# Output weights in 28 contiguous rows per partition, the attention output re-laid through HBM, and five last transfers: a decode step of attention and a gated feed-forward on one core

## The chip, the cores and the metric

The kernel runs on one core of a Trainium2 chip. The metric is the device time of one execution in microseconds (us), the median of several runs; lower is better.

## The reference

One token `x` (1 x 448) is normalised (mean and variance, no weights) to `xn`, and three terms are added: `x`, an attention over a cache, and a block `B` of the mixture kind that, with one token to choose from, always chooses it.

```
q = (xn @ wq) in 16 heads of 256;  k, v = caches of 8 heads, 65536 positions, 256 wide (two q heads share one)
p = softmax(q . k / 16) over the 65536 positions;   o = p @ v          (16 x 256)
A = o.reshape(4096) @ wo                                                (wo: 4096 x 448)
B = xn + sigmoid(xn @ w_r) * ((silu(xn @ w_gate) * (xn @ w_up)) @ w_down)
out = x + A + B
```

Everything in HBM is bf16. Keys and values are 268 MB each, of 549 MB that are read in all; each byte is used once.

## The kernel before, in words

**Units.** The 65536 positions of a head lie 512 to a partition. A unit is 128 of them per partition (8.4 MB of keys or values), so a head has `U` = 4 units, and there are `NU` = 32 key units and 32 value units. Three slots of one large tile `ring` hold units: keys alternate between slots 0 and 1, values come through slot 2. Within a unit, TensorE transposes keys (`k_T`), multiplies them with q (`k_QK`), and the scores are turned back to positions on partitions (`k_JT`); after a head's last key unit the softmax follows, and then four units of values (`pe_V`), which lag the keys by one head. `NT` = 28 value units belong to heads 0 to 6, the last four (`NT` to `NT + 3`) to head 7, in `ending()`.

**Queues.** Each engine has a list of its operations in program order, written out by hand: `O` records an operation, `W` a wait for another one, `item` a transfer that SP issues, with what SP waits for ahead of it. SP issues all large transfers in one order. Its last ones are: value unit `NT` to slot 0; gate and up weights (`wg`), down weights (`wd`) and output weights of heads 0 to 6 (`wo`) to slot 2, which holds no values at that time; value unit `NT + 1` to slot 1, `NT + 2` to slot 0; unit `NT + 3` to slot 2, in the parts of `LAST`, after `SUM`, the last use of the weights there; the rest of `wo` (`wx`, after `HT`); and head 7's output weights in three parts (`wo_end`, waits `we0` to `we2`).

**The attention output.** For heads 0 to 6, `oT_all` (and its sum over units, `oT_f`) has feature 2p + f of a head on partition p. The weights `wo` come with four consecutive rows of a head's 512 on each partition (`wo_rows`: "(h p f) n -> p h f n"), so each of the two q heads of a pair takes half of the partitions. `REGROUP` brings `oT_f` into that layout: 16 small products with strided columns of the identity, each to a half of the partitions. `OTH` copies the result to `oT_h` in bf16. `ATTN` then adds 26 products of a column of `oT_h` with 448 columns of `wo` in `ps_a`; the last two rows per partition of head 6 come later as `wx` and are added in `FIN_X`.

**Behind it on TensorE**: `FFN1G`, `FFN1` (gate and up), `HTP`, `FFN2` (down); on VectorE `YS`, `YX`, and `SUM`, which adds `ps_a`. Then the values of unit `NT + 1`, `FIN_BASE`, units `NT + 2` and `NT + 3`. Between the parts of `NT + 3`, `WARM` puts products whose results are not used. The last `DIRECT` parts are multiplied with the values as the stationary side ("direct"), so that `OB` (the copy of `ps_o`) can be made from the parts before. Then `OT`, `OTSB`, `FIN_X` and the three `FIN` with head 7's weights, `RESULT`, and the transfer of the output.

All TensorE products are recorded at line 413, in a helper, and all transfers at line 903; so readings go by tile: `ps_q` with `oT_h` is ATTN, `ps_t` with `xnT_sb` FFN1, `ps_t` with `hT_sb` FFN2, `ps_o` the values. `kt_all L826` on DVE is SUM.

Of the kernel before, what the change touches and what calls it, by code (L numbers as in the profile page):

```python
# [4 lines left out]
BF16 = mybir.dt.bfloat16  # L5
# [5 lines left out]
NKT = 4  # L11
NSLOT = 3
CH = 64
HC = 2
LAST = [64, 32, 16, 8, 4, 4]
DIRECT = 2
NF = 4
WARM = {0: (5, 512), 1: (2, 512), 2: (1, 512), 3: (1, 256)}
ACT_M = (3,)
TORD = (3, 0, 1, 2)  # L20

# [1 line left out]
def bass_parallel_sum__gqa_block_cached__moe_arch_mod__decode_kernel(  # L23
# [20 lines left out]
    P = 128  # L44
    _, Hkv, Sk, Dh = A_k_cache.shape
    D = A_x.shape[-1]
    HqDh = A_wq.shape[1]
    Hq = HqDh // Dh
    rep = Hq // Hkv
    F = B_w_gate.shape[1]  # L50
    NH = Dh // P
# [3 lines left out]
    FK = F // P  # L55
# [20 lines left out]
    SLOT = HC * CH * Dh  # L76
    HALF = CH * Dh
    WQN, WGN, WDN, WON = RP * HqDh // 2, RP * F, FH * D, rep * NH * D
    FO = rep * NH
    WOA = (Hkv - 1) * WON  # L80
    WEN = WOA + WGN + 2 * WDN
    assert WEN + 2 * D <= SLOT
# [3 lines left out]
    def S_(name, shape, dtype):  # L86
        t = nc.sbuf_tensor(name, shape, dtype)
        sb.append(t)
        return t.__enter__()

    ring = S_("ring", [P, NSLOT * SLOT], BF16)
    kt_all = S_("kt_all", [P, NKT * 8 * P], BF16)
# [3 lines left out]
    wo_all = slots[2][:, 0:WOA]  # L96
# [35 lines left out]
    rs = S_("rs", [P, NH, rep], FP32)  # L132
    oT_all = S_("oT_all", [P, NH, NT, rep], FP32)
    oT_f = S_("oT_f", [P, NH, Hkv - 1, rep], FP32)
    oT_h = S_("oT_h", [P, FO, Hkv - 1], BF16)
    KB = 2 * FB
    sg_sb = [kt_all[0:2, c * KB:(c + 1) * KB].bitcast(FP32) for c in range(2)]
    h_sb = kt_all[0:2, 2 * KB:3 * KB]
# [1 line left out]
    DQ = D // NF  # L140
    FROWS = 32 * (NF - 1) + 1
    res_bf = kt_all[0:FROWS, 3 * KB + 2 * D:3 * KB + 2 * D + DQ]
    wo_x = kt_all[:, 2 * KB:2 * KB + WON // 2]
    assert WON // 2 <= KB and WON <= 2 * KB and 3 * KB + 2 * D + DQ <= NKT * 8 * P
    hT_sb = S_("hT_sb", [P, FH, 2], BF16)
    ob_sb = S_("ob_sb", [P, 2 * Dh], BF16)
    oT_sb = S_("oT_sb", [P, NH, rep], BF16)
# [19 lines left out]
    ps_m = PS_("ps_m", [P, 512], FP32)  # L167
    C_XNT, C_BC, C_TOT, C_OT, C_Q, C_BIG = 0, 16, 18, 22, 28, 64
    C_HT = C_Q
    assert C_Q + NH * Hq + 4 <= C_BIG and C_HT + FK <= C_BIG and C_BIG + P <= 512  # L170

    sems = {}
    handles = []
# [4 lines left out]
        sems[name] = s.__enter__()  # L178
        return name

    for n_ in ["pe", "act", "dve", "pool", "qk", "jt", "evq", "exp", "pc", "qc", "sc", "w0", "out", "wq", "wg", "wo", "wd", "we0", "we1", "we2", "wx", "half0", "half1"]:
        SEM(n_)
    for i in range(NTB):
        SEM(f"ev{i}")
# [23 lines left out]
    def W(e, *key):  # L208
        put(e, "w", key, None, None)
# [3 lines left out]
    def O(e, key, fn, sem=None, n=1):  # L213
        key = key if isinstance(key, tuple) else (key,)
        if not ghost[0]:
            weight[key] = n
        put(e, "o", key, fn, sem or e)
# [21 lines left out]
    def item(key, parts, need=()):  # L239
        for n in need:  # L240
            W("sp", *n)
        for ap, src, sem in parts:
            semtot[sem] = semtot.get(sem, 0) + 16
            items[key] = (sem, semtot[sem])
            prog["sp"].append(("d", here[0], ("DMA", key, len(prog["sp"])), (ap, src), sem))
# [22 lines left out]
    def wo_view(t):  # L268
        return t.rearrange("p (i f n) -> p i f n", i=rep, f=NH)

    def wo_rows(h0, h1):

        return A_wo[h0 * rep * Dh:h1 * rep * Dh, :].rearrange("(h p f) n -> p h f n", p=P, f=FO)

    def wo_at(h, f):
        return wo_all[:, (h * FO + f) * D:(h * FO + f + 1) * D]

    def k_item(u):
        need = [("FREE", u - 2)] if u >= 2 else ()
# [13 lines left out]
    for t in range(1, NT):  # L293
        v_item(t)
        if t + U + 1 < NU:
# [1 line left out]
    slot_item("v", NT, 0, None, [("FREE", NU - 2)])  # L297
    item("wg", [(wg_area[:, 0:WGN // 2], flat_src(B_w_gate, F), "wg"), (wg_area[:, WGN // 2:WGN], flat_src(B_w_up, F), "wg")], [("VFREE", NT - 1)])
    item("wd", [(wd_area.rearrange("p (s x) -> p s x", s=2), B_w_down.rearrange("(s p t) n -> p s (t n)", s=2, p=P), "wd"), (x_again, A_x[0], "wd")])
    HL = Hkv - 2  # L300
    item("wo", [(wo_all[:, 0:HL * WON].rearrange("p (h x) -> p h x", h=HL), wo_rows(0, HL).rearrange("p h f n -> p h (f n)"), "wo"),
                (wo_all[:, HL * WON:HL * WON + WON // 2], wo_rows(HL, HL + 1)[:, 0, 0:FO // 2, :].rearrange("p f n -> p (f n)"), "wo")])
    slot_item("v", NT + 1, 1, None, [("FREE", NU - 1)])
    slot_item("v", NT + 2, 0, None, [("VFREE", NT)])
    slot_item("v", NT + 3, 2, [("last%d" % k if k < len(LAST) - 1 else "slot2", J) for k, J in enumerate(LAST)], [("SUM",)])
    item("wx", [(wo_x, wo_rows(HL, HL + 1)[:, 0, FO // 2:FO, :].rearrange("p f n -> p (f n)"), "wx")], [("HT",)])
    ENDS = [(0, 0, NH), (1, 0, 1), (1, 1, NH)]
    for k, (i, f0, f1) in enumerate(ENDS):
        item(("wo_end", k), [(wo_view(wo_end)[:, i, f0:f1, :], wo_src()[:, i, f0:f1, :], "we%d" % k)])
# [102 lines left out]
    def mm(*a, **k):  # L412
        return pe.matmul(*a, **k)  # L413
# [242 lines left out]
    def pe_attn():  # L656
        W("dve", "OTSB", NT - 1)
        for hf in range(NH):
            O("dve", ("OTF", hf), lambda it, hf=hf: nc.vector.tensor_reduce(
                out=oT_f[:, hf, :, :], in_=oT_all[:, hf, :, :].rearrange("p (h t) i -> p h i t", t=U), axis=AX.X, op=ALU.add))  # L660
        W("dve", "OTF", NH - 1)
        W("pe", "OTF", NH - 1)
        HN = Hkv - 1

        def regroup(it):

            for i in range(rep):
                for r in range(rep):
                    for hf in range(NH):
                        c = C_BIG + (r * NH + hf) * HN  # L670
                        ins = mm(ps_m[i * P // rep:(i + 1) * P // rep, c:c + HN], lhsT=ident_f[:, r:P:rep], rhs=oT_f[:, hf, :, i],
                                 start=True, stop=True, tile_position=(0, i * P // rep))
            return ins

        O("pe", "REGROUP", regroup)
        W("dve", "REGROUP")
        O("dve", "OTH", lambda it: nc.vector.tensor_copy(
            out=oT_h[:, :, :], in_=ps_m[:, C_BIG:C_BIG + FO * HN].rearrange("p (f h) -> p f h", f=FO)))
        W("pe", "OTH")
        W_item("pe", "wo")  # L680
        todo = [(h, f) for h in range(HN) for f in range(FO) if h < HN - 1 or f < FO // 2]
        O("pe", "ATTN", lambda it: [mm(ps_a, lhsT=oT_h[:, f, h:h + 1], rhs=wo_at(h, f),
                                       start=(h, f) == todo[0], stop=(h, f) == todo[-1]) for h, f in todo][-1])

    def pe_ffn1():
        W_item("pe", "wg")
# [101 lines left out]
    def fin(rows, o, col, first=False, last=False):  # L788
        for g in range(NF):
            ins = mm(ps_s[32 * g:32 * g + 1, 0:DQ], lhsT=col, rhs=rows[:, o + g * DQ:o + (g + 1) * DQ], start=first,  # L790
                     stop=last, tile_position=(0, 32 * g), skip_group_check=True)
        return ins
# [5 lines left out]
    def ending():  # L798
        here[0] = ("S", 1)
        T = NU - 1  # L800
        n = NU * SETS
        k_JT(n - 2)
        k_QK(n - 1)
        k_JT(n - 1)
        pe_m1t(T)
        pe_bc(T)
        W("pe", "OTSB", NT - 1)
        values(NT)
        pe_tot(NT)
        pe_attn()  # L810
        pe_ffn1()
        pe_ffn_hT()
        pe_ffn2()
        W_item("dve", "wd")
        O("dve", "XN_AGAIN", lambda it: nc.vector.tensor_scalar(out=xn_again, in0=x_again, scalar1=stat[0:1, 7:8], scalar2=stat[0:1, 4:5],
                                                                op0=ALU.add, op1=ALU.mult))
        W("dve", "XN_AGAIN")
        W("dve", "FFN2")
        W("dve", "ATTN")
        W("dve", "SIG")  # L820
        O("dve", "YS", lambda it: nc.vector.scalar_tensor_tensor(  # L821
            out=sum_f, in0=ps_y, scalar=stat[0:1, 6:7], in1=xn_again, op0=ALU.mult, op1=ALU.add))
        W("dve", "YS")
        O("dve", "YX", lambda it: nc.vector.tensor_tensor(out=sum_f, in0=sum_f, in1=x_again, op=ALU.add))
        W("dve", "YX")
        O("dve", "SUM", lambda it: nc.vector.tensor_tensor(out=sum_f, in0=ps_a, in1=sum_f, op=ALU.add))  # L826
        values(NT + 1)
        W("pe", "SUM")
        W("pe", "SCOPY", T)

        O("pe", "FIN_BASE", lambda it: fin(sum_f, 0, ones_f[0:1, 0:1], first=True))
        O("pe", "OT_ZERO", lambda it: mm(ps_m[0:P, C_OT:C_OT + NH * rep], lhsT=s2[0][:, 0:P], rhs=zero_bf[:, 0:NH * rep], start=True, stop=True,
                                         skip_group_check=True))
        values(NT + 2)
        values(NT + 3)
        dve_ob(T)
        pe_oT(T)
        W_item("pe", "wx")

        def fin_x(it):  # L840
            for f in range(FO // 2):
                ins = fin(wo_x, f * D, oT_h[:, FO // 2 + f, HL:HL + 1])
            return ins

        O("pe", "FIN_X", fin_x)
        W("pe", "OTSB", T)
        for k, (i, f0, f1) in enumerate(ENDS):
            W_item("pe", ("wo_end", k))

            def f(it, k=k, i=i, f0=f0, f1=f1):  # L850
                for hf in range(f0, f1):
                    ins = fin(wo_end, (i * NH + hf) * D, oT_sb[:, hf, i:i + 1], last=k == len(ENDS) - 1 and hf == f1 - 1)
                return ins

            O("pe", ("FIN", k), f)
        W("dve", "FIN", len(ENDS) - 1)
        O("dve", "RESULT", lambda it: nc.vector.tensor_copy(out=res_bf, in_=ps_s[0:FROWS, 0:DQ]))
        W("sp", "RESULT")
        prog["sp"].append(("d", here[0], ("OUT", 0), (out[0, 0].rearrange("(g n) -> g n", g=NF), res_bf[0:FROWS:32, :]), "out"))
# [272 lines left out]
```

## Time and profile before

| | |
|---|---|
| median of 3 runs | 1277.01 us (1277.01 to 1277.2) |
| profiled execution | 1278.14 us |
| its span, first to last instruction | 1275.5 us |
| read from HBM | 549.03 MB, 430 GB/s over the span |
| granted TensorE clock, mean | 0.881 |
| busy: PE, DVE, ACT | 965.2, 570.5, 436.1 us |
| DMA packets | 12890 |

Times are on the profiled execution's own axis, from the start of its span. PE is TensorE, DVE VectorE, ACT ScalarE; a queue is a list of transfers (q1 is fed by SP, q10 by ACT), which 16 DMA engines work off in packets. "idle before" and square brackets name what an engine waited for last. Rows of the DMA view give packets, megabytes and the time that the packets took as a share of 16 engines over the window.

### The profile page before, as it was taken

How to read it: one execution, taken by the hardware profiler on the slowest of the kernel's cores; microseconds unless marked ns; L12 is line 12 of the kernel's file. 1: busy time of each engine (PE TensorE's matmuls, PEld its weight loads, DVE VectorE, ACT ScalarE, POOL GpSimd, SP SyncE). 2: the span in 40 equal slices, each digit the busy share in tenths (PEclk: the TensorE clock that was granted, in tenths of full speed). 3: DMA queues.
4: the chain of work that ended last, by engine and by line, in shares of the span. 5: the costliest groups of instructions: out<-in, count | busy, mean ns of one | idle time of the engine just before them, and what ended most of it. 6: DMA issues, size and time to landing. Idle time of an engine off the chain costs nothing.

```text
span 1275.5 us, 23552 instructions
## 1 busy us (share of the span) xinstructions
PE 965.2 (76%) x9760; PEld 632.0 (50%) x9760; DVE 570.5 (45%) x1078; ACT 436.1 (34%) x655; POOL 8.0 (1%) x38
## 2 busy tenths in 40 slices
PE   3998988678777779777778776787777698777664
PEld 3676655445444455444455444554454555444331
DVE  4665544445434455343454444453444544444310
ACT  1554433244322434233333243343333334322300
POOL 2000000000000000000000000000000000000000
PEclk9998998889888889887898888898888988888877
DMA  9999999999999999999999999999999999999998
GB/s 404 430 435 433 441 430 434 432 430 444 430 432 436 428 440 434 432 434 432 430 442 432 432 436 430 438 436 430 434 432 430 442 432 432 436 430 436 418 438 357
DMA packets 12890, 549.20 MB, mean 431 GB/s; under 512 B 1355, under 2 KB 1998, under 8 KB 3406
## 3 DMA queue, kind: packets, MB, share of 16 engines
q1 hardware_dynamic: 12874, 549.04, 99.7%
q8 instruction: 8, 0.13, 0.0%
q14 instruction: 4, 0.03, 0.0%
q10 hardware_dynamic: 4, 0.00, 0.0%
HBM read 549.03 MB, written 0.00 MB: 430 GB/s over the span
## 4 chain that ended last, share of the span: by engine, by line
DMA 78%; PE 18%; ACT 2%; issue 1%; DVE 1%; SPq 0%; ACTq 0%; DVEq 0%
DMA ring<-in_A_v_cache_dram 68%; PE ps_o L413 12%; DMA ring<-in_A_k_cache_dram 5%; PE ps_t L413 3%; DMA kt_all<-in_A_wo_dram 3%; DMA ring<-in_A_wo_dram 2%; PE ps_q L413 2%; ACT kt_all L474 2%; PE ps_m L413 1%; SPq L903 0%; DVE kt_all L472 0%; ACT S_sb L555 0%; DVE kt_all L715 0%; PE ps_s L413 0%; DVE kt_all L821 0%
## 5 line engine op out<-in xcount | busy, mean ns | idle before, releaser
L413 PE MATMUL ps_t<-ident_f,ring 128*128 128x128 f32 x4096 | 591.2, 287 | 78.0 <-DMA ring<-in_A_k_cache_dram 56.4
L472 DVE COPY kt_all<-ps_t 128x1024 bf16<-128x1024 bf16 x768 | 487.3, 685 | 291.4 <-PE ps_q L413 286.3
L413 PEld LDWEIGHTS ps_t<-ident_f,ring 128*128 128x128 f32 x4096 | 454.9, 144 | 230.2 <-issue 135.1
L474 ACT ACTIVATE kt_all<-ps_t 128x1024 bf16<-128x1024 bf16 x256 | 261.9, 1023 | 502.2 <-PE ps_q L413 502.1
L413 PE MATMUL ps_o<-ring,p_sb 128*4 128x512 bf16 x2044 | 179.6, 513 | 201.7 <-DMA ring<-in_A_v_cache_dram 197.4
L413 PEld LDWEIGHTS ps_o<-ring,p_sb 128*4 128x4 bf16 x2044 | 54.6, 102 | 289.6 <-issue 264.1
L413 PE MATMUL ps_q<-kt_all,q_cur 128*2 128x512 bf16 x2056 | 164.3, 396 | 0.4 <-DVE kt_all L472 0.4
L496 ACT ACTIVATE s<-ps_q 98x512 bf16<-98x512 f32 x257 | 151.6, 590 | 1.3 <-PE ps_q L413 1.3
L578 DVE RECIPROCAL rs<-ps_m 128x4 f32<-128x4 f32 x29 | 5.3, 183 | 271.6 <-PE ps_m L413 271.6
L565 ACT ACTIVATE p_sb<-S_sb 128x128 bf16<-128x128 bf16 x64 | 18.9, 307 | 262.6 <-PE ps_o L413 262.3
L413 PEld LDWEIGHTS ps_s<-sel_bf,s 128*128 128x128 bf16 x1032 | 64.6, 98 | 5.2 <-ACT s L496 1.9
L413 PE MATMUL ps_s<-sel_bf,s 128*128 128x8 bf16 x1032 | 63.6, 167 | 1.3 <-ACT s L496 1.3
L631 DVE CAST ob_sb<-ps_o 100x512 bf16<-100x512 f32 x29 | 20.1, 692 | 92.4 <-PE ps_o L413 92.4
L413 PEld LDWEIGHTS ps_q<-kt_all,q_cur 128*2 128x2 bf16 x2056 | 26.4, 79 | 44.5 <-issue 44.5
L413 PEld LDWEIGHTS ps_m<-rowsum,ones_f 128*128 128x128 f32 x58 | 12.4, 266 | 23.5 <-issue 23.5
L474 ACT ACT_TABLE_LOAD x7 | 9.0, 1283 | 26.0 <-PE ps_q L413 26.0
L525 DVE TENSOR_REDUCE m1p<-S_sb (+1 forms) x33 | 13.9, 422 | 4.4
L413 PE MATMUL ps_m<-rowsum,ones_f 128*128 128x4 f32 x58 | 14.9, 328 | 0.0
L523 DVE CAST S_sb<-ps_s 128x256 f32 (+1 forms) x33 | 13.7, 415 | 1.9 <-PE ps_s L413 1.9
L555 ACT ACTIVATE S_sb<-S_sb,negmax 128x512 bf16<-128x512 bf16 x16 | 13.2, 851 | 3.2 <-DVE negmax L549 3.2
L413 PE MATMUL ps_m<-diag,ones_f 2*128 2x2 f32 x58 | 11.2, 260 | 3.8 <-DVE diag L540 1.1
L413 PEld LDWEIGHTS ps_m<-diag,ones_f 2*128 2x128 f32 x58 | 8.7, 187 | 10.7 <-DVE diag L540 10.7
(95 smaller groups left out, 132.8 us busy)
## 6 DMA issues: line engine op xcount, KB each, us to landing
ring<-in_A_k_cache_dram SPq DMA_DIRECT2D x10, 4096.0 KB, 28.7
ring<-in_A_v_cache_dram SPq DMA_DIRECT2D x1, 4096.0 KB, 26.5
ring<-in_A_wq_dram SPq DMA_DIRECT2D x1, 3584.0 KB, 11.3
ring<-in_A_wo_dram SPq DMA_DIRECT2D x1, 2688.0 KB, 27.6
ring<-in_A_v_cache_dram SPq DMA_DIRECT2D x1, 2048.0 KB, 30.7
ring<-in_B_w_gate_dram SPq DMA_DIRECT2D x1, 1568.0 KB, 16.2
ring<-in_B_w_up_dram SPq DMA_DIRECT2D x1, 1568.0 KB, 19.6
ring<-in_B_w_down_dram SPq DMA_DIRECT2D x1, 1568.0 KB
```

The lines of the kernel that those rows point to most:

```text
L413: return pe.matmul(*a, **k)
L472: O(e, ("EV", s, m), lambda it: nc.vector.tensor_copy(out=kt[:, :], in_=tb[:, :]), f"ev{m}")
L474: O(e, ("EV", s, m), lambda it: nc.scalar.activation(out=kt[:, :], in_=tb[:, :], func=ACTF.Copy), f"ev{m}")
L496: O("act", ("EVQ", s), lambda it: nc.scalar.activation(out=s2[s % 2][0:QROWS, :], in_=ps_q[0:QROWS, :], func=ACTF.Copy), "evq")
L523: O("dve", ("SCOPY", u), lambda it: nc.vector.tensor_copy(out=S_sb[:, at(it, SBN), :], in_=ps_sn), "sc")
L525: O("dve", ("SMAX", u), lambda it: nc.vector.tensor_reduce(out=m1p[:, :, at(it, 1)], in_=S_sb[:, at(it, SBN), :].rearrange("p n i -> p i n ...
L555: O("act", ("EXP", h, i), lambda it, i=i: nc.scalar.activation(out=S_sb[:, :, i], in_=S_sb[:, :, i], func=ACTF.Exp, bias=negmax[:, i:i + 1 ...
L565: O("act", ("PC", t, c), lambda it: nc.scalar.activation(out=p_sb[:, c, :, :], in_=S_sb[:, n:n + CH, :], func=ACTF.Copy), "pc")
L578: O("dve", ("RS", t), lambda it: nc.vector.reciprocal(out=rs[:, :, :], in_=ps_m[0:P, C_TOT:C_TOT + NH * rep]))
L631: O("dve", ("OB", t), lambda it: nc.vector.tensor_copy(out=ob_sb[0:OROWS, :], in_=ps_o[0:OROWS, :]))
```

## The change

The output weights of heads 0 to 6 (3584 rows) are read as 28 contiguous rows per partition: 26 of them in `wo`, one transfer, and the last two in `wx`. Element 28p + f of the attention output then has to be on partition p. `REGROUP` and `OTH` are replaced: two transposes (`OTROW`) put `oT_f` in 14 rows of 256, `OROW` copies them to `o_row` (a part of `kt_all`) in bf16, ACT writes them to `o_flat` in HBM, waits for that (`oh0`), and reads them back as 128 runs of 28 elements into `oT_h` (`oh1`), for which TensorE waits ahead of `ATTN`. The last value unit comes in five parts and not six: 64, 32, 16, 8 and 8 positions per partition, of which the last is "direct" (before: two of 4). One of the `WARM` entries goes.

```diff
-LAST = [64, 32, 16, 8, 4, 4]
-DIRECT = 2
+LAST = [64, 32, 16, 8, 8]
+DIRECT = 1
+WX = 2
-WARM = {0: (5, 512), 1: (2, 512), 2: (1, 512), 3: (1, 256)}
+WARM = {0: (5, 512), 1: (2, 512), 2: (1, 512)}
...
-    FO = rep * NH
+    FR = (Hkv - 1) * rep * Dh // P
...
-    oT_h = S_("oT_h", [P, FO, Hkv - 1], BF16)
+    oT_h = S_("oT_h", [P, FR], BF16)
+    o_flat = nc.dram_tensor("o_flat", [(Hkv - 1) * rep, Dh], BF16).ap()
...
-    wo_x = kt_all[:, 2 * KB:2 * KB + WON // 2]
+    wo_x = kt_all[:, 2 * KB:2 * KB + WX * D]
+    o_row = kt_all[0:(Hkv - 1) * rep, 2 * KB:2 * KB + Dh]
...
-        return A_wo[h0 * rep * Dh:h1 * rep * Dh, :].rearrange("(h p f) n -> p h f n", p=P, f=FO)
+        return A_wo[0:(Hq - rep) * Dh, :].rearrange("(p f) n -> p f n", f=FR)[:, f0:f1, :].rearrange("p f n -> p (f n)")
...
-    item("wo", [(wo_all[:, 0:HL * WON].rearrange("p (h x) -> p h x", h=HL), wo_rows(0, HL).rearrange("p h f n -> p h (f n)"), "wo"),
-                (wo_all[:, HL * WON:HL * WON + WON // 2], wo_rows(HL, HL + 1)[:, 0, 0:FO // 2, :].rearrange("p f n -> p (f n)"), "wo")])
+    item("wo", [(wo_all[:, 0:(FR - WX) * D], wo_rows(0, FR - WX), "wo")])
...
-    item("wx", [(wo_x, wo_rows(HL, HL + 1)[:, 0, FO // 2:FO, :].rearrange("p f n -> p (f n)"), "wx")], [("HT",)])
+    item("wx", [(wo_x, wo_rows(FR - WX, FR), "wx")], [("HT",)])
...
-        W("pe", "OTF", NH - 1)
-        HN = Hkv - 1
-        def regroup(it):
...
-        O("pe", "REGROUP", regroup)
-        W("dve", "REGROUP")
-        O("dve", "OTH", lambda it: nc.vector.tensor_copy(
-            out=oT_h[:, :, :], in_=ps_m[:, C_BIG:C_BIG + FO * HN].rearrange("p (f h) -> p f h", f=FO)))
-        W("pe", "OTH")
+        HR = (Hkv - 1) * rep
+        for hf in range(NH):
+            W("pe", "OTF", hf)
+            O("pe", ("OTROW", hf), lambda it, hf=hf: mm(ps_m[0:HR, C_BIG + hf * P:C_BIG + (hf + 1) * P],
+                                                        lhsT=oT_f[:, hf, :, :].rearrange("p h i -> p (h i)"), rhs=ident_f[:, :],
+                                                        is_transpose=True, start=True, stop=True))
+        W("dve", "OTROW", NH - 1)
+        O("dve", "OROW", lambda it: nc.vector.tensor_copy(
+            out=o_row.rearrange("r (p f) -> r f p", f=NH), in_=ps_m[0:HR, C_BIG:C_BIG + NH * P].rearrange("r (f p) -> r f p", f=NH)))
+        W("act", "OROW")
+        for k, (dst, src) in enumerate(((o_flat, o_row), (oT_h[:, :], o_flat.rearrange("r d -> (r d)").rearrange("(p f) -> p f", f=FR)))):
+            items["oh", k] = ("oh%d" % k, 16)
+            prog["act"].append(("d", here[0], ("DMA", "oh", k), (dst, src), "oh%d" % k))
+            if k == 0:
+                W("act", "DMA", ("oh", 0))
+        W("pe", "DMA", ("oh", 1))
         W_item("pe", "wo")
-        todo = [(h, f) for h in range(HN) for f in range(FO) if h < HN - 1 or f < FO // 2]
-        O("pe", "ATTN", lambda it: [mm(ps_a, lhsT=oT_h[:, f, h:h + 1], rhs=wo_at(h, f),
-                                       start=(h, f) == todo[0], stop=(h, f) == todo[-1]) for h, f in todo][-1])
+        O("pe", "ATTN", lambda it: [mm(ps_a, lhsT=oT_h[:, f:f + 1], rhs=wo_all[:, f * D:(f + 1) * D],
+                                       start=f == 0, stop=f == FR - WX - 1) for f in range(FR - WX)][-1])
...
-            for f in range(FO // 2):
-                ins = fin(wo_x, f * D, oT_h[:, FO // 2 + f, HL:HL + 1])
+            for f in range(WX):
+                ins = fin(wo_x, f * D, oT_h[:, FR - WX + f:FR - WX + f + 1])
```

More of the change, by code (lines that the diff above doesn't have):

```diff
@@ L142, in bass_parallel_sum__gqa_block_cached__moe_arch_mod__decode_kernel @@
     res_bf = kt_all[0:FROWS, 3 * KB + 2 * D:3 * KB + 2 * D + DQ]
-    wo_x = kt_all[:, 2 * KB:2 * KB + WON // 2]
-    assert WON // 2 <= KB and WON <= 2 * KB and 3 * KB + 2 * D + DQ <= NKT * 8 * P
+    wo_x = kt_all[:, 2 * KB:2 * KB + WX * D]
+    o_row = kt_all[0:(Hkv - 1) * rep, 2 * KB:2 * KB + Dh]
+    assert WX * D <= KB and Dh <= KB and WON <= 2 * KB and 3 * KB + 2 * D + DQ <= NKT * 8 * P
     hT_sb = S_("hT_sb", [P, FH, 2], BF16)
@@ L169, in bass_parallel_sum__gqa_block_cached__moe_arch_mod__decode_kernel @@
     C_HT = C_Q
-    assert C_Q + NH * Hq + 4 <= C_BIG and C_HT + FK <= C_BIG and C_BIG + P <= 512
+    assert C_Q + NH * Hq + 4 <= C_BIG and C_HT + FK <= C_BIG and C_BIG + NH * P <= 512
     sems = {}
@@ L179, in SEM @@
         return name
-    for n_ in ["pe", "act", "dve", "pool", "qk", "jt", "evq", "exp", "pc", "qc", "sc", "w0", "out", "wq", "wg", "wo", "wd", "we0", "we1", "we2", "wx", "half0", "half1"]:
+    for n_ in ["pe", "act", "dve", "pool", "qk", "jt", "evq", "exp", "pc", "qc", "sc", "w0", "out", "wq", "wg", "wo", "wd", "we0", "we1", "we2", "wx", "oh0", "oh1", "half0", "half1"]:
         SEM(n_)
@@ L269, in wo_view, with wo_rows @@
         return t.rearrange("p (i f n) -> p i f n", i=rep, f=NH)
-    def wo_rows(h0, h1):
-        return A_wo[h0 * rep * Dh:h1 * rep * Dh, :].rearrange("(h p f) n -> p h f n", p=P, f=FO)
-    def wo_at(h, f):
-        return wo_all[:, (h * FO + f) * D:(h * FO + f + 1) * D]
+    def wo_rows(f0, f1):
+        return A_wo[0:(Hq - rep) * Dh, :].rearrange("(p f) n -> p f n", f=FR)[:, f0:f1, :].rearrange("p f n -> p (f n)")
     def k_item(u):
@@ L299, in bass_parallel_sum__gqa_block_cached__moe_arch_mod__decode_kernel @@
     item("wd", [(wd_area.rearrange("p (s x) -> p s x", s=2), B_w_down.rearrange("(s p t) n -> p s (t n)", s=2, p=P), "wd"), (x_again, A_x[0], "wd")])
-    HL = Hkv - 2
-    item("wo", [(wo_all[:, 0:HL * WON].rearrange("p (h x) -> p h x", h=HL), wo_rows(0, HL).rearrange("p h f n -> p h (f n)"), "wo"),
-                (wo_all[:, HL * WON:HL * WON + WON // 2], wo_rows(HL, HL + 1)[:, 0, 0:FO // 2, :].rearrange("p f n -> p (f n)"), "wo")])
+    item("wo", [(wo_all[:, 0:(FR - WX) * D], wo_rows(0, FR - WX), "wo")])
     slot_item("v", NT + 1, 1, None, [("FREE", NU - 1)])
@@ L661, in pe_attn @@
         W("dve", "OTF", NH - 1)
-        W("pe", "OTF", NH - 1)
-        HN = Hkv - 1
-        def regroup(it):
[L667 to L673, printed above, removed]
-        O("pe", "REGROUP", regroup)
-        W("dve", "REGROUP")
-        O("dve", "OTH", lambda it: nc.vector.tensor_copy(
-            out=oT_h[:, :, :], in_=ps_m[:, C_BIG:C_BIG + FO * HN].rearrange("p (f h) -> p f h", f=FO)))
-        W("pe", "OTH")
+        HR = (Hkv - 1) * rep
[14 more added lines that the diff above has]
+        W("pe", "DMA", ("oh", 1))
         W_item("pe", "wo")
-        todo = [(h, f) for h in range(HN) for f in range(FO) if h < HN - 1 or f < FO // 2]
-        O("pe", "ATTN", lambda it: [mm(ps_a, lhsT=oT_h[:, f, h:h + 1], rhs=wo_at(h, f),
-                                       start=(h, f) == todo[0], stop=(h, f) == todo[-1]) for h, f in todo][-1])
+        O("pe", "ATTN", lambda it: [mm(ps_a, lhsT=oT_h[:, f:f + 1], rhs=wo_all[:, f * D:(f + 1) * D],
+                                       start=f == 0, stop=f == FR - WX - 1) for f in range(FR - WX)][-1])
     def pe_ffn1():
```

## The prediction

> **What bounds the kernel now.** I read the page first: spans, queues and the chain that ended last.
>
> ```profile
> span 1275.5 us, 23552 instructions
> PE 965.2 (76%) x9760; PEld 632.0 (50%) x9760; DVE 570.5 (45%) x1078; ACT 436.1 (34%) x655; POOL 8.0 (1%) x38
> q1 hardware_dynamic: 12874, 549.04, 99.7%
> DMA 78%; PE 18%; ACT 2%; issue 1%; DVE 1%; SPq 0%; ACTq 0%; DVEq 0%
> ```
>
> One queue, the one that SP feeds, holds the 16 DMA engines for 99.7% of the span. So the kernel is a stream of transfers: what a change does to the time is what it does to the stream, either work of the engines taken away, or a moment in which the queue is empty. The profiled execution took 1278.14 us, 2.64 beyond its span; the median of the runs shown is 1277.01, 1.13 below it. I work out shifts of the span and put them on the median.
>
> The change sits in the last 70 us, so next I read the chain in order of time there, the PE and DVE timeline, and SP's waits.
>
> ```profile
> 1184.07 28.92 DMA ring<-in_A_wo_dram
> ...
> 1234.24 0.62 DVE kt_all L826
> ...
> 1239.33 33.21 DMA kt_all<-in_A_wo_dram
> ```
>
> ```profile
> 1207.16 0.92 PE L413 MATMUL ps_m<-oT_f,ident_f 128*64 128x7 f32 x16 [0.49 <-DVE oT_f L659]
> 1213.12 7.62 PE L413 MATMUL ps_q<-ring,oT_h 128*1 128x448 bf16 x26 [5.04 <-DMA ring<-in_A_wo_dram]
> ...
> 1251.83 5.59 PE L413 MATMUL ps_o<-ring,p_sb 128*4 128x512 bf16 x64 [15.19 <-DMA ring<-in_A_v_cache_dram]
> ```
>
> ```profile
> 1206.81 0.30 DVE L659 TENSOR_REDUCE oT_f<-oT_all 128x14 f32<-128x56 f32 x2
> 1208.19 0.19 DVE L677 CAST oT_h<-ps_m 128x28 bf16<-128x28 f32 x1 [1.08 <-PE ps_m L413]
> ```
>
> ```profile
> SPq L903 <- DVE kt_all L826: 28.1, 1, 28.1
> ```
>
> Two slacks are to be seen. ATTN (the 26 products at 1213.12) waits 5.04 us for the weights, while its other input was ready at 1208.19 + 0.19 = 1208.4. And behind ATTN, FFN1 and FFN2 comes SUM (L826), which ends at 1234.24 + 0.62 = 1234.86; SP waits 28.1 us for it before it may refill slot 2 with the last unit of values. That refill isn't needed before the units ahead of it in the queue are through: the second last one lands at 1251.83.
>
> **The stream: weights in longer runs.** The cost of a packet comes from windows of the DMA view that hold one size alone: 1205.6 to 1209.6 (3584 bytes), 7 to 9 (28672 bytes), 600 to 1000 (65536 bytes, with 335 semaphore packets).
>
> ```profile
> q1 hardware_dynamic: 451, 1.62, 102.0%
> q1 hardware_dynamic: 27, 0.77, 89.6%
> DMA packets 2981, 173.41 MB, mean 434 GB/s; under 512 B 335, under 2 KB 335, under 8 KB 335
> q1 hardware_dynamic: 2981, 173.41, 100.2%
> ```
>
> Share x 16 engines x window, over the packets: 1.020 x 16 x 4 / 451 = 0.145 us; 0.896 x 16 x 2 / 27 = 1.062; 1.002 x 16 x 400 / 2646 = 2.42. The last two give 37.0 ns per 1000 bytes; a 3584-byte packet needs 0.133 by that, so a packet costs 0.012 on top. Before, an engine has 8 partitions x 6 heads = 48 packets of 3584 bytes and 8 of 1792 (estimate 0.078): 6.96 + 0.62 = 7.58. After, 8 of 26 x 896 = 23296 bytes (estimate 0.87): 6.96. Gain 0.6. Two last transfers of 4 rows become one of 8: 8 packets fewer, 0.1. So the stream is worth 0.7, less what the trip puts on the engines.
>
> **What goes and comes ahead of the trip.** REGROUP and OTH (0.92 and 0.19) go. Two transposes come, of the kind of the 0.27 row below, and a copy to 14 rows of 256, nearest to the 0.42 row.
>
> ```profile
> 1197.10 0.27 PE L413 MATMUL ps_m<-ident_f,m 128*2 128x128 f32 x1 [1.17 <-DVE m L529]
> 1195.96 0.42 DVE L523 CAST S_sb<-ps_s 128x256 bf16<-128x256 f32 x1 [1.90 <-PE ps_s L413]
> ```
>
> OTF ends at 1207.1, the transposes at about 1207.6, the copy at 1208.2: as OTH before.
>
> **The trip.** ACT issues a write of 14 rows, waits for it, and issues a read of 128 runs of 56 bytes: 8 packets and a semaphore packet on each of 16 engines, since each 128-partition transfer here has one packet per partition. ATTN waits for the read. This is the added wait. Behind it on PE stand ATTN, FFN1, FFN2 and the values of unit NT+1, and so SUM, and SP's refill behind that; on ACT the sigmoids and later copies of p, which wait for PE anyway.
>
> What such a transfer costs beside a full SP queue, the trace shows once: at the start ACT issues two loads of 896 bytes, the second into a running stream of 28672-byte packets. ACT's issues, and who waited for the second:
>
> ```profile
> 0.73 0.52 ACTq L903 DMA_DIRECT2D ring<-in_A_x_dram  x1
> 1.28 0.21 ACTq L903 DMA_DIRECT2D ring<-in_B_w_r_dram  x1
> 7.31 1.65 DVE L356 CAST ring<-ring 1x448 f32<-1x448 bf16 x1 [3.12 <-DMA ring<-in_B_w_r_dram]
> ```
>
> The DMA view in the windows 1.5 to 1.8, 1.8 to 5.8, 5.8 to 5.9, 5.9 to 6.94 and 6.94 to 7:
>
> ```profile
> q10 hardware_dynamic: 2, 0.00, 2.4%
> ...
> DMA packets 49, 1.40 MB, mean 351 GB/s; under 512 B 0, under 2 KB 0, under 8 KB 0
> ...
> q10 hardware_dynamic: 1, 0.00, 2.6%
> ...
> DMA packets 14, 0.40 MB, mean 386 GB/s; under 512 B 0, under 2 KB 0, under 8 KB 0
> ...
> q10 hardware_dynamic: 1, 0.00, 0.9%
> ```
>
> q10 is ACT's queue. The first load has its data and its semaphore packet together in one window, some 0.9 us after its issue; nothing was running yet. The second starts its data only at 5.8, 4.5 us after its issue: 3.6 more. And its semaphore packet comes not behind the data but in 6.94 to 7, about 1.06 us later: one 28672-byte packet of the other queue stood between. That is what I take for the trip: the two queues take turns packet by packet, and a tiny packet waits for a whole packet of SP's queue each time. From about 1210 that queue carries 65536-byte packets, 2.42 us each.
>
> Write: 1208.2 + 0.9 + 3.6 (I keep the measured time, though the packets are longer) + 2.42 to the semaphore packet + 0.35 from the semaphore packet to who waits (7.31 less about 6.96, in the last window) = 1215.5. Read: 0.1 to issue + 0.9 + 3.6 + 8 turns x 2.42 = 19.4 + 0.35 = 24.3, so ATTN starts at 1239.8 in place of 1213.1. SUM follows 21.7 us after ATTN's start (1234.86 less 1213.12), at 1261.5. First packets of the last unit 0.03 + 0.9 later (SP's issue below): 1262.5.
>
> ```profile
> 1234.88 1.09 SPq L903 DMA_DIRECT2D ring<-in_A_v_cache_dram  x2
> ```
>
> The queue has run dry by then: the unit before landed at 1251.83, its last packet 0.35 earlier, 1251.5. So the last unit starts 11.0 late, plus some 0.6 for restarting an idle stream (49 packets in 4 us at the start: estimate 1.26 each against 1.06, three of them), less 0.1 for the merged transfers; the weights' 0.6 is lost in the gap. **Shift +11.5, 1288.5 us.** The bounds: if no packets are waited for but the one under way (1.2, in the write 0.4 and 0.9), ATTN starts at 1232.7 and the shift is +4.5; if three 65536-byte packets stand ahead of each transfer (7.3), ATTN starts at 1247.2 and it is +19.
>
> By the Trainium skill ("DMA: Bandwidth & Descriptors", Queues, rings and completion order) an engine changes queues only after a whole packet, typically 9 to 17 descriptors; the trace, with a load's data and semaphore 1.06 us apart, speaks against it here.
>
> **The tail.** One transfer of 8 rows means 16 direct products behind the last landing in place of 8.
>
> ```profile
> 1271.47 0.35 PE L413 MATMUL ps_m<-p_sb,ring 128*128 128x2 bf16 x8 [0.30 <-DMA ring<-in_A_v_cache_dram]
> 1272.67 0.76 PE L413 MATMUL ps_s<-kt_all,oT_sb 128*1 128x112 bf16 x16 [0.36 <-DMA kt_all<-in_A_wo_dram]
> ```
>
> They add 0.35, under the wait for the end weights (direct products end 1271.82, FIN's second half starts 1272.67); without that cover at most 0.35. The dropped warming product ran in a wait: nothing.
>
> **The rivals.** *The trip is short* (25%). If an engine serves ACT's 8 packets in one turn, the write takes 0.9 + 3.6 + 0.35 and the read 0.1 more: ATTN starts at 1218, SUM ends at 1239.8, 11.7 before the queue would run dry. Then only the stream counts: -0.7, and the trip's packets cost at most 9 x 0.042 (2.6% of 16 x 0.1) = 0.4: -0.3 to -0.7, 1276.5 us. The point from which it decides: SUM has to end by about 1248, so ATTN to start by 1226, a trip under 18 us. For it: the trace never shows several ACT packets to one engine. Against it: the semaphore packet above. This is also what the skill's rule on whole packets would make of it; and the same page (Anatomy of one DMA) puts a DMA's fixed cost at about 2 us, by which the trip took 4 us and the sum were the same -0.5.
>
> *The trip outlasts the stream* (7%). If more than one packet goes by per turn, the read ends only once SP's queue is empty: 1251.5 + 0.35, ATTN at 1251.9, SUM 1273.6, restart 1274.5, shift +23.5, 1300.5 us.
>
> *The long runs don't pay, or are cut up* (within the cases above): they are 0.6 in all, hidden in the gap or lost in the noise.
>
> **How the numbers follow.** The turn-by-turn trip has 66%, and with it 1288.5; its own range is 1282 to 1296 from the bounds. The short trip has 25%, the long one 7%, 2% are left for a gain that I don't see. The range for 8 in 10 must take in the short trip: 1276 to 1296. A measurement of this kernel can tell about 0.2%, 2.6 us, from no change: the short trip counts as no change. Faster 0.02, same 0.25, slower 0.73.
>
> **What would show it.** Right: ATTN waits for a transfer from the flat copy, some 25 us longer than before; the read's packets lie over some 20 us; PE starts FFN1 near 1247; the DMA share falls to nothing for about 11 us near 1251 to 1262; SP waits some 55 us for SUM. Wrong: ATTN at 1213 to 1226 and no gap; or the gap there and the trip's time elsewhere, in the write and not in the read's turns. Packets of 23296 bytes at 0.87 us confirm the stream's term in every case.

## The result, and the profile after

The changed kernel takes 1287.62 us (median of 4 runs, 1285.93 to 1291.21) against 1277.01 before: 10.6 us more, a ratio of 1.0085 with a 95% interval of 1.0072 to 1.0098. The forecast was 1288.5. The profiled execution took 1287.91 us, its span 1286.3. Instructions of the changed kernel carry line numbers two to four lower than before: products are L411, transfers L899, SUM L822.

The page and the chain that ended last (start, duration, what it was):

```profile
span 1286.3 us, 23522 instructions
q1 hardware_dynamic: 11946, 549.03, 98.9%
q10 hardware_dynamic: 176, 0.02, 0.0%
```

```profile
1207.82 8.47 DMA o_flat<-kt_all
1216.31 23.57 DMA oT_h<-o_flat
1239.92 6.65 PE ps_q L411 x26
1246.56 5.31 PE ps_t L411 x28
...
1258.37 0.63 DVE kt_all L822
...
1263.23 20.75 DMA kt_all<-in_A_wo_dram
```

Before, this stretch of the chain began with the weights' transfer. Now it is the two halves of the trip: 8.47 us for the write, 23.57 for the read, and ATTN behind them. The timeline of TensorE and SP's waits say the same from the other side:

```profile
1206.85 0.39 PE L411 MATMUL ps_m<-ident_f,oT_f 128*14 128x128 f32 x2 [0.37 <-DVE oT_f L657]
1239.92 6.65 PE L411 MATMUL ps_q<-ring,oT_h 128*1 128x448 bf16 x26 [32.67 <-DMA oT_h<-o_flat]
```

```profile
SPq L899 <- DVE kt_all L822: 52.5, 1, 52.5
```

ATTN waits 32.67 us for the trip (5.04 for the weights before), SP 52.5 for SUM (28.1 before). What that does to the stream is in the DMA view. Its rows in two windows, 1223.0 to 1227.84 (two turns of 2.42 us, in the middle of the read) and 1250.8 to 1259.9:

```profile
q1 hardware_dynamic: 32, 2.10, 100.2%
q10 hardware_dynamic: 32, 0.00, 0.5%
...
DMA packets 1, 0.02 MB, mean 2 GB/s; under 512 B 0, under 2 KB 0, under 8 KB 0
q8 instruction: 1, 0.02, 0.9%
```

In the first, 16 engines start 32 packets of SP's queue and 32 of ACT's: one of each per engine and turn. The large ones are not slowed, their share is that of a full queue. In the second window not one packet of SP's queue starts: the engines moved nothing for about 9 us but one piece of code. Engine by engine, the last packets end between 1248.5 and 1250.8, and the refill's first ones start between 1259.97 and 1260.6: 10.5 us without work on the mean engine, against a span that is 10.8 longer. That gap is the loss.

### The profile page after: what moved, and what is told of

It reads as the page before. It is cut to its first block, busy times and chain, and to the rows that moved or that the text cites. A ratio compares the mean times of both kernels' runs of the same rounds, so it can differ in the third digit from the quotient of the medians.

```text
span 1286.3 us, 23522 instructions
## 1 busy us (share of the span) xinstructions
PE 951.0 (74%) x9745; PEld 622.9 (48%) x9745; DVE 570.3 (44%) x1078; ACT 436.1 (34%) x655; POOL 8.0 (1%) x38
## 3 DMA queue, kind: packets, MB, share of 16 engines
q1 hardware_dynamic: 11946, 549.03, 98.9%
## 4 chain that ended last, share of the span: by engine, by line
DMA 76%; PE 19%; ACT 2%; issue 1%; DVE 1%; SPq 0%; ACTq 0%; DVEq 0%
DMA ring<-in_A_v_cache_dram 68%; PE ps_o L411 13%; DMA ring<-in_A_k_cache_dram 5%; PE ps_t L411 3%; PE ps_q L411 2%; DMA oT_h<-o_flat 2%; ACT kt_all L472 2%; DMA kt_all<-in_A_wo_dram 2%; PE ps_m L411 1%; DMA o_flat<-kt_all 1%; SPq L899 0%; DVE kt_all L470 0%; ACT S_sb L553 0%; DVE kt_all L711 0%; DVE m1p L523 0%
## 5 line engine op out<-in xcount | busy, mean ns | idle before, releaser
L411 PE MATMUL ps_t<-ident_f,ring 128*128 128x128 f32 x4096 | 584.7, 284 | 82.2 <-DMA ring<-in_A_k_cache_dram 58.4
L411 PEld LDWEIGHTS ps_t<-ident_f,ring 128*128 128x128 f32 x4096 | 448.7, 143 | 233.6 <-issue 134.1
L411 PE MATMUL ps_o<-ring,p_sb 128*4 128x512 bf16 x2044 | 178.0, 508 | 193.9 <-DMA ring<-in_A_v_cache_dram 189.6
L411 PEld LDWEIGHTS ps_o<-ring,p_sb 128*4 128x4 bf16 x2044 | 54.0, 102 | 280.9 <-issue 253.5
L411 PE MATMUL ps_q<-kt_all,q_cur 128*2 128x512 bf16 x2056 | 163.4, 394 | 0.3 <-DVE kt_all L470 0.3
L411 PEld LDWEIGHTS ps_s<-sel_bf,s 128*128 128x128 bf16 x1032 | 64.0, 97 | 5.0 <-ACT s L494 1.9
L411 PE MATMUL ps_s<-sel_bf,s 128*128 128x8 bf16 x1032 | 63.3, 167 | 1.3 <-ACT s L494 1.3
L411 PEld LDWEIGHTS ps_q<-kt_all,q_cur 128*2 128x2 bf16 x2056 | 26.4, 79 | 44.6 <-issue 44.6
L411 PE MATMUL ps_q<-ring,oT_h 128*1 128x448 bf16 x26 | 6.6, 426 | 32.7 <-DMA oT_h<-o_flat 32.7
L411 PEld LDWEIGHTS ps_m<-rowsum,ones_f 128*128 128x128 f32 x58 | 12.1, 261 | 22.2 <-issue 22.2
L411 PEld LDWEIGHTS ps_q<-ring,oT_h 128*1 128x1 bf16 x26 | 2.5, 97 | 36.6 <-DMA oT_h<-o_flat 32.9
L411 PE MATMUL ps_m<-rowsum,ones_f 128*128 128x4 f32 x58 | 14.7, 323 | 0.0
```

## The experiments

Every ratio below is against the kernel before, run beside it, whose median lay between 1277.2 and 1277.6. The diffs are shortened: `...` marks what is left out, and a line that names operations in brackets, without code, stands for their code.

**Parts alone.** The kernel before with `LAST = [64, 32, 16, 8, 8]`, `DIRECT = 1` and without the fourth `WARM`.

```diff
-LAST = [64, 32, 16, 8, 4, 4]
-DIRECT = 2
+LAST = [64, 32, 16, 8, 8]
+DIRECT = 1
-WARM = {0: (5, 512), 1: (2, 512), 2: (1, 512), 3: (1, 256)}
+WARM = {0: (5, 512), 1: (2, 512), 2: (1, 512)}
```

> The five last transfers alone (8 and 8 positions in place of 8, 4 and 4, one direct part, one warming product fewer); weights and re-lay as before. My theory: eight packets fewer per engine, -0.1 us, 1276.9. Rival (the tail pays for sixteen direct products behind the last landing, and this edit has a part in the loss): 1277.3 or more.

Measured: 1277.34 us, ratio 0.9998 (0.9989 to 1.0007). No part of the loss; the 0.1 forecast is too small to be seen. (The rival's 1277.3 is reached, but the kernel before took 1277.28 beside it.)

**Rows without the trip.**

```diff
-        (OTROW, OROW, write, read)
+        O("pe", "REGROUP", regroup)
+        O("dve", "OTH", lambda it: nc.vector.tensor_copy(
+            out=oT_h[:, :].rearrange("p (f h) -> p f h", f=FO), in_=ps_m[:, C_BIG:C_BIG + FO * HN].rearrange("p (f h) -> p f h", f=FO)))
+        W("pe", "OTH")
```

> The 28 contiguous rows and the five parts, without the trip: the attention output is regrouped on TensorE as before, which puts wrong elements against the weights. My theory: ATTN starts when the weights land, as before, no gap in the queue, and the stream gains 0.7 us: 1276.3. Rival (the long rows are the loss, by slower reads or by what they do to the queue): 1280 to 1288.

Measured: 1276.84 us, ratio 0.9995 (0.9986 to 1.0004). The interval takes in no change; the trace shows that the stream is indeed shorter. The transfer of the output is issued at 1273.26, at 1273.79 with the parts alone. These are SP's rows of the timeline, of the rows and of the parts:

```profile
1273.26 0.62 SPq L900 DMA_DIRECT2D out_dram<-kt_all  x1
```

```profile
1273.79 0.61 SPq L903 DMA_DIRECT2D out_dram<-kt_all  x1
```

So the long rows bring 0.5 in the one profiled execution, of 0.6 forecast. Over all runs the span says the same: its median is 1274.9 us (11 runs) against 1275.5 in the kernel before (27 runs). They aren't the loss.

**The trip alone**, added to the kernel before (old rows, old parts); the read goes to a spare tile, for which ATTN waits too.

```diff
+        (OTROW, OROW, write as in the change; the read into oT_x)
         O("pe", "REGROUP", regroup)
         ...
         W("pe", "OTH")
+        W("pe", "DMA", ("oh", 1))
```

> The trip through HBM alone, added to the kernel before: weights, REGROUP and six parts as before, the trip's result goes to a spare tile, and ATTN waits for it as well. My theory: the whole loss is here. ATTN starts near 1240 as in the changed kernel, the queue runs dry near 1251 and takes up again near 1260: 1287 to 1289 us. Rival (rows or parts are the loss): within 1 us of 1277.

Measured: 1290.32 us, ratio 1.0101 (1.0086 to 1.0117). Timeline:

```profile
1239.51 6.76 PE L418 MATMUL ps_q<-ring,oT_h 128*1 128x448 bf16 x26 [30.78 <-DMA oT_x<-o_flat]
```

The whole loss is in this part of the change, with ATTN at 1239.5 as in the changed kernel. (The median is 1.3 us above the range that I gave. In the profiled execution, 1289.04 us, 1.0 of it stands at the very end: the span ends 2.7 us behind the output's issue, 1.7 in the changed kernel, of which more below. Why its four runs spread from 1288.25 to 1291.78 stays open.)

**The size of a turn.** In the changed kernel, units `NT + 1` and `NT + 2` come in four transfers each, so that SP's packets are 16384 bytes during the trip. (The second edit keeps the "direct" products to unit `NT + 3`.)

```diff
-    slot_item("v", NT + 1, 1, None, [("FREE", NU - 1)])
-    slot_item("v", NT + 2, 0, None, [("VFREE", NT)])
+    slot_item("v", NT + 1, 1, [("va%d" % k, SBN // 4) for k in range(4)], [("FREE", NU - 1)])
+    slot_item("v", NT + 2, 0, [("vb%d" % k, SBN // 4) for k in range(4)], [("VFREE", NT)])
...
-            direct = k > len(parts) - 1 - DIRECT and len(parts) > 1
+            direct = k > len(parts) - 1 - DIRECT and t == NT + 3
```

> The changed kernel with the value units NT+1 and NT+2, which fill SP's queue during the trip, each read in four transfers of 32 positions (packets of 16384 bytes in place of 65536). My theory (ACT's packets take turns with SP's, one by one): a turn is 0.61 us and not 2.42; the write takes some 5 us, the read some 8 (0.9 to the first turn, one or two packets ahead, 8 turns = 4.9), ATTN starts near 1221 and SUM ends near 1241, no gap; the shorter packets cost the stream 2 x 8 x 3 x 0.012 = 0.6: 1276.7 to 1277.2. Rival (the trip's time is latency of HBM or of the small runs, whatever stands beside them): ATTN near 1240 and 1287 as before.

Measured: 1277.25 us, ratio 0.9998 (0.9988 to 1.0007): the loss is gone. Chain, and the DMA view from 1216 to 1221.2:

```profile
1207.06 5.44 DMA o_flat<-kt_all
1212.53 9.15 DMA oT_h<-o_flat
1221.72 7.87 PE ps_q L411 x26
```

```profile
q1 hardware_dynamic: 151, 2.21, 100.2%
q10 hardware_dynamic: 144, 0.01, 1.9%
```

The same 144 packets of the read now start within 5.2 us. Nothing of the trip was changed, only what its packets take turns with. This rules out that the trip is slow by HBM's latency or by the smallness of its runs.

**The number of turns.** The read in two transfers of half the columns: twice the packets, the same bytes.

```diff
-        for k, (dst, src) in enumerate(((o_flat, o_row), (oT_h[:, :], o_flat...))):
+        o_cols = o_flat.rearrange("r d -> (r d)").rearrange("(p f) -> p f", f=FR)
+        for k, (dst, src) in enumerate(((o_flat, o_row), (oT_h[:, 0:FR // 2], o_cols[:, 0:FR // 2]), (oT_h[:, FR // 2:FR], o_cols[:, FR // 2:FR]))):
...
         W("pe", "DMA", ("oh", 1))
+        W("pe", "DMA", ("oh", 2))
```

> The changed kernel with the read in two transfers of half the columns, issued one behind the other: 16 data packets of 28 bytes and two semaphore packets per engine in place of 8 and one, the same bytes. My theory: 17 turns of 2.42 us behind the first, 41 us from near 1220, which is beyond the end of SP's queue near 1251; there the rest passes at once. ATTN starts near 1251.5, SUM ends near 1270.5, the refill near 1271.5: 11.5 more than the changed kernel, 1299. Rival (latency): two transfers overlap, the time stays at 1287.

Measured: 1302.36 us, ratio 1.0194 (1.0179 to 1.021). Chain, and the DMA view from 1240 to 1248 and from 1251.2 to 1274.4:

```profile
1206.07 5.37 DMA o_flat<-kt_all
1211.85 39.96 DMA oT_h<-o_flat
1251.91 7.46 PE ps_q L411 x26
```

```profile
q1 hardware_dynamic: 54, 3.54, 102.3%
q10 hardware_dynamic: 53, 0.00, 0.4%
...
DMA packets 1, 0.02 MB, mean 1 GB/s; under 512 B 0, under 2 KB 0, under 8 KB 0
```

ATTN starts at 1251.9, half a microsecond from the forecast, once SP's queue is empty and the rest of the small packets pass at once. It is the bound that the prediction's third case gave for a trip that outlasts the stream. The time is 3.4 above the expected 1299. Of that 2.6 is the way from ATTN's start to SUM's end: 21.6 us (1251.91 to 1272.87 + 0.61), where I had put 19.

**The read alone.** The write is left out, and the read takes its elements from the output weights, so ATTN's products are of other numbers.

```diff
-        for k, (dst, src) in enumerate(((o_flat, o_row), (oT_h[:, :], o_flat...))):
+        o_cols = A_wo[0:FR * P // D, :].rearrange("r d -> (r d)").rearrange("(p f) -> p f", f=FR)
+        for k, (dst, src) in ((1, (oT_h[:, :], o_cols)),):
...
-            if k == 0:
-                W("act", "DMA", ("oh", 0))
```

> The changed kernel without the write half of the trip: ACT issues the read alone, of 3584 elements of the output weights in place of the attention output, so the products of ATTN are of other numbers. My theory: the read's issue moves from 1216.3 to about 1207.5, its eight turns of 2.42 us stay (19.4, a turn or two of 0.87 among them while the weights still come), and ATTN starts at 1230 to 1231.5. SUM follows 19 to 22 later, 1249 to 1253.5, the refill 1 us behind it, where the queue runs dry from 1248.4 to 1250.8: a gap of 0 to 4 us, 1277 to 1280. Rival (the write to HBM is the slow half, and the read is short without it): ATTN near 1215, no gap, 1276.5.

Measured: 1279.03 us (1277.86 to 1282.39), ratio 1.0021 (1.0012 to 1.0031). Timeline, ACT's queue and TensorE:

```profile
1206.43 0.36 ACTq L897 DMA_DIRECT2D oT_h<-in_A_wo_dram  x1
```

```profile
1230.04 6.70 PE L410 MATMUL ps_q<-ring,oT_h 128*1 128x448 bf16 x26 [24.18 <-DMA oT_h<-in_A_wo_dram]
```

The read takes 23.6 us from issue to ATTN, as with the write ahead of it; SUM ends at 1248.56 + 0.61 = 1249.2 (L820 here), and that is just where the queue runs dry, engine by engine from 1248.5 to 1250.9. ATTN starts 9.9 us sooner than in the changed kernel, and 8.8 of the 10.6 come back. So up to about this point a longer wait of ATTN costs nothing (with the smaller packets it started at 1221.7, in the kernel before at 1213.1, and the times are the same), and beyond it nearly the whole of it.

**Another order.** The trip is left as it is; FFN1, FFN2 and the values of unit `NT + 1` go ahead of ATTN, and `o_row` lies where they write nothing.

```diff
         (OTROW, OROW, write, read)
-        ATTN
         pe_ffn1(); pe_ffn_hT(); pe_ffn2()
         ... YS, YX
+        values(NT + 1)
+        ATTN
         SUM
-        values(NT + 1)
```

> The changed kernel with another order on TensorE behind the trip's start: FFN1, FFN2 and the values of unit NT+1 come first, ATTN and SUM after them. The trip, its transfers and their packets are untouched. My theory: the trip still takes about 32 us and ATTN still starts near 1240, but only ATTN and SUM (some 8 us, not 19) stand between it and SP's refill: SUM near 1248, the refill's packets near 1249, where the first engine runs dry at 1248.5 and the last at 1250.8. 1276.4 us, up to 1277. Rival (the trip's packets themselves slow the stream): about 1287 as before this edit.

Measured: 1277.62 us, ratio 1.0003 (0.9994 to 1.0012). Timeline:

```profile
1239.77 5.08 PE L413 MATMUL ps_q<-ring,oT_h 128*1 128x448 bf16 x26 [3.09 <-DMA oT_h<-o_flat]
```

The trip ends at 1239.8 as before, and costs nothing, since only ATTN and SUM (1244.89 + 0.61 = 1245.5, L828 here) stand behind it. The 0.6 us of the longer rows didn't show. The end of the span is why, in this execution: the output's transfer is issued at 1273.07, 0.71 sooner than before, but the span ends 2.7 us later and not 1.7, with a transfer of 8 KB of code in between (DMA view from 1273.07 to 1275.8):

```profile
1273.07 0.61 SPq L904 DMA_DIRECT2D out_dram<-kt_all  x1
```

```profile
q14 instruction: 1, 0.01, 1.3%
q1 hardware_dynamic: 8, 0.00, 0.2%
```

**The same with 247 instructions on VectorE**, and **the kernel before with 248**: in the first the clearing of one score buffer goes to GpSimd, in the second another one is done twice. (247 and 248 count VectorE's program as it is written down, loops once; the traces don't show that count.)

```diff
-        O("dve", "s2z0", lambda it: v.memset(s2[0][:, :], 0.0), "ev2")
+        O("pool", "s2z0", lambda it: v.memset(s2[0][:, :], 0.0), "ev2")
...
         W("act", "S2Z")
+        W("act", "KZ")
```

```diff
+        O("dve", "S2Z_0", lambda it: v.memset(s2[1][:, :], 0.0))
+        W("dve", "S2Z_0")
         O("dve", "S2Z", lambda it: v.memset(s2[1][:, :], 0.0))
```

> The kernel of the run order with one operation fewer on VectorE: the clearing of one score buffer goes to GpSimd. In the run order the last products ended 0.7 us sooner than in the kernel before, but the output's transfer took from its issue to the end 2.7 us in place of 1.7, with an 8 KB instruction transfer beside it; VectorE's program has 248 instructions there and in the run trip, 247 in the kernels that end in 1.7. My theory: at 248 the end of VectorE's program lies in a block of code that is fetched only then, and the end waits 1.0 us for it. At 247 the end takes 1.7 again and the whole is 0.7 us below the kernel before. Rival (the slower end comes of the order of the work): as the run order, 0.3 us above the kernel before.

Measured: 1276.89 us, ratio 0.9995 (0.9986 to 1.0004); output issued at 1273.45, end of span at 1275.1, 1.65 later.

> The kernel before with one more small clearing on VectorE at the very start, which repeats the one that is there (248 instructions in place of 247). Theory of the code block: the last 1.7 us become 2.7, the whole 1.0 us slower, about 1278.2. Rival: no change, since the operation lies in an idle time of VectorE.

Measured: 1277.85 us, ratio 1.0003 (0.9994 to 1.0012); output issued at 1274.28, end of span at 1277.1, 2.8 later, with the code transfer in between. The span behaves as the theory has it, both times. The whole time doesn't: 0.3 us more and not 1.0, which is inside the interval. Over all runs the padded kernel's span is 0.9 us longer (mean of 11 runs 1276.45, of the 27 of the kernel before 1275.56), and what its time has beyond the span is 0.5 shorter (1.5 against 2.0): about half of what the span gains at its end is missing behind it. The DMA view of the padded kernel from 1274.28 to 1277.1, and of the kernel before from 1275.5, the end of its span, to 1278:

```profile
q14 instruction: 1, 0.01, 1.2%
...
q14 instruction: 1, 0.01, 1.0%
```

The kernel before has this transfer too, but 2.5 us behind the output's issue, when its span has ended; with one instruction more it comes 1.2 us behind it. That fits a fetch that is only moved across the end of the span, but no run shows that it is the cause. Whether 247 instructions are worth anything stays open, and so does whether the reordered kernel is faster than the kernel before: by the medians 0.7 us, by the interval it can't be told from none.

## Why the prediction was right, point by point

*The stream bounds, and a gap in it is the loss.* Right: the queue's share fell from 99.7% to 98.9% of a longer span, and the gap is there.

*Turns, packet by packet.* Right, and the core of it: 32 packets against 32 in two turns, 9 us of read where a turn is 0.61 us, 40 us where there are twice as many. The write of the changed kernel has the finest case. On 8 of its 14 engines a 65536-byte packet stood between its data and its semaphore packet, which start some 2.44 us apart; on the other 6 the packet in between was the 4-byte semaphore packet that ends the weights' transfer, and they start 0.03 us apart. The rule of whole packets that the prediction weighed ("DMA: Bandwidth & Descriptors", Queues, rings and completion order, of the Trainium skill) doesn't describe these transfers: every run of 56 bytes waited for a turn of its own. Nor does the fixed cost of about 2 us on that page of the Trainium skill (Anatomy of one DMA, whose heading gives it for transfers that GpSimd issues) price these, which ACT issues: the read took 23.57.

*The trip's sum.* ATTN was forecast for 1239.8 and started at 1239.92. That it is so close is luck: the write was issued 0.4 sooner than forecast (1207.82), took 8.5 (7.3 forecast), and the read 23.6 (24.3), and the three misses cancel. To the first packet both carried 0.9 + 3.6 = 4.5 us, taken from a load beside packets of 28672 bytes; it was 3.5 in both (1207.82 to 1211.37, 1216.31 to 1219.85). The write lost more than that: its first packets lie over 2 us (1211.37 to 1213.39), each at the end of a packet under way, and only then comes the turn. That what stands ahead is a time and not a number of packets, which the prediction only chose, the runs bear out: the read's first packet starts 3.5 us after its issue beside packets of 65536 bytes (1216.31 to 1219.8) and of 16384 (1212.53 to 1216.0). In the changed kernel all 144 of the read lie between 1219.8 and 1239.5:

```profile
q10 hardware_dynamic: 144, 0.01, 0.5%
```

*From ATTN to SUM*: 21.7 forecast from the trace of before, 19.1 measured (1239.92 to 1258.37 + 0.63). This is the term that was mis-sized most. Of the 2.6 us, ATTN itself has 1.0 (7.62 before at a mean granted clock of 0.66, 6.65 now at 0.76) and FFN2 most of the rest. The windows of FFN2 in the kernel before, the changed one and the one with the doubled read (columns: length, busy time and count of PE, PEld, DVE, ACT, POOL, then the granted clock, the DMA share and GB/s):

```profile
1228.20:1232.80 4.60, 4.51 (x21) 1.82 (x25) 0.23 (x1) 0.00 (x0) 0.00 (x0) 0.63 1.05 456
```

```profile
1254.00:1257.00 3.00, 2.89 (x28) 1.33 (x32) 0.25 (x1) 0.00 (x0) 0.00 (x0) 1.00 0.03 5
```

```profile
1267.00:1271.50 4.50, 4.50 (x28) 1.64 (x30) 0.06 (x1) 0.00 (x0) 0.00 (x0) 0.62 0.02 4
```

The same 14 products behind the same short waits met a granted clock of 0.63, 1.00 and 0.62. The prediction took a duration over with the clock that it happened to have. In these traces the clock is 0.50 or 1.00 and changes only at the borders of stretches of 3.41 us. Here are the stretch that ends where FFN2 begins, in the kernel before, the one behind it, and in the changed kernel the last one that ends ahead of FFN2:

```profile
1225.13:1228.54 3.41, 1.66 (x14) 0.86 (x13) 1.61 (x5) 0.00 (x0) 0.00 (x0) 1.00 0.80 346
1228.54:1231.95 3.41, 3.41 (x11) 1.17 (x10) 0.00 (x0) 0.00 (x0) 0.00 (x0) 0.50 1.02 442
```

```profile
1249.95:1253.37 3.42, 2.03 (x14) 0.82 (x12) 2.15 (x4) 0.26 (x1) 0.00 (x0) 1.00 0.00 0
```

Behind 1.66 or 1.67 us of TensorE's work in such a stretch the clock fell at FFN2 (the kernel before, its padded form, the rows, the smaller packets, the doubled read), behind 2.02 or 2.03 it stayed (the changed kernel, the parts, the trip alone, the read alone). So in these nine traces it goes by where the borders fall in the work. Busy time alone isn't the rule: at 1259.26 in the kernel before the clock stays behind a stretch with 1.57. The Trainium skill ("TensorE: Matmul & The Clock Gate", Part 1) has the clock follow TensorE's activity in windows of about 3.4 us that run freely and don't begin anew with a kernel; the traces agree with that in the length of the stretches. It may also be why the changed kernel's runs spread over 5 us and those of the kernel before over 0.4 (1.6 in 27 later runs), since only now does this way stand on the path. That is not shown, and one run speaks against it: the way is on the path with the doubled read too, and its four runs lie within 0.34 us.

*Restart to end.* The refill's first packets start 1.0 after SUM, as forecast. From there to the end it took 1.8 more than the prediction's 24.5 (1262.5 to 1275.5 + 11.5). The restart's 0.6, which it had, is there (packets of 32768 bytes took 1.295 us on the mean against 1.220, nearly all of it in the first packet of each engine, 1.78). On top of it the first transfer reaches the 16 engines over 0.6 us (10 of the first 16 packets start between 1259.9 and 1260.1, all by 1260.65), and a transfer of code of 16 KB stands among the last parts:

```profile
q1 hardware_dynamic: 217, 0.45, 97.0%
q8 instruction: 1, 0.02, 5.4%
```

(The window is 1279.8 to 1281.) The engine that carries it is busy with it for 1.04 us (5.4% of 16 x 1.2). Such transfers were there before too, but then the engines were some 2 us apart, and one that wasn't last could bear it; after the gap they start together. That this delays the end is a reading of one trace. The two misses, -2.6 and +1.8, nearly cancel: +11.5 forecast, +10.6 measured, +10.8 in the span. The mechanism was right; that the sum came within 1 us of the time is in part luck.

*The 0.7 us of the stream.* Rows: 0.5 of 0.6 in the trace (packets of 23296 bytes took 0.87 us, as estimated), and in the changed kernel hidden in the gap, as forecast. Parts: nothing seen of 0.1.

*The tail.* The sixteen direct products took 0.55 us and ended ahead of the last weights, as forecast.

*The rivals.* The short trip (25%) would have needed 18 us or less; it came to 32. With 16384-byte packets it came to 14.7 and the loss was gone. Its point of decision, ATTN by 1226, was placed some 3 us too early: with the read alone ATTN started at 1230.04 and SUM still ended at 1249.2, since the way between them took 19.1 and not 21.7. The long one (7%) is what the doubled read did, with ATTN at 1251.91 (1251.9 forecast).

## What to carry to other kernels

A small transfer on a second queue beside a saturated one doesn't cost its bytes: here each of its packets waited for one packet of the other queue, so its time was some 3.5 us to the first packet and then the number of its packets per engine times the other queue's packet time. Before a trip through HBM is put on the path, look what size of packets will be under way at that moment, and what the end of the trip holds up; shorter packets there, or independent work put between the trip and its user, took the whole cost away here. And a gap in a saturated stream is priced from the point at which the queue runs dry, not from the wait itself. A duration that is taken over from one trace carries that trace's clock with it: 4.5 us of FFN2 became 2.8.

## What the runs showed of the hardware that was not expected

- From the issue to a transfer's first packet it took 3.4 to 3.9 us beside a full queue in the trip's writes and reads, whether the other queue's packets were 65536 or 16384 bytes, and 4.5 at the start of the kernel before; with idle engines it was 0.9. Why, no run shows.
- The granted clock changed only at borders 3.41 us apart, and the same 14 products took 2.8 us in the changed kernel, 4.5 in the kernel before, by where those borders fell.
- The end of the span depended on one instruction more on VectorE: at 247 it followed the output's issue by 1.6 to 1.7 us, at 248 by 2.7 to 2.8, with an 8 KB code transfer in that time (three kernels at 248 and eight at 247). About half of that came back behind the span in the padded kernel.
